# Gated mix of sliding attention and a SwiGLU layer: the tail's queues, its late rows and output, and the place of the gates

## The chip, the core and the metric

The kernel runs on one core of one Trainium2 chip. A core has TensorE (PE, matmuls), VectorE (DVE), ScalarE (ACT), GpSimd (POOL) and SyncE (SP), each with an instruction stream of its own that it executes in order. A transfer (DMA) is issued by an engine's queue, here SyncE's or GpSimd's, and carried by 16 DMA engines. An instruction that waits for a semaphore holds up everything behind it on its engine. The metric is device time in microseconds (us). Three runs gave 838.3, 838.88 and 845.08; the median is 838.88.

## The reference

Inputs in float32: x is 2048 by 512, there are 32 heads of width 16, the attention window is 256 back, the hidden width of the second layer is 1792.

```
q, k, v = split(x @ wqkv)                        # 32 heads of 16
p = softmax(mask(q k^T / 4))                     # 0 <= i - j < 256
a = (p v) @ wo
b = (silu(x @ w_gate) * (x @ w_up)) @ w_down
g = sigmoid(sum(x * gate_w, -1))                 # one number for each row
out = g * a + (1 - g) * b
```

## The kernel before

Products in full precision are made of three matmuls: each operand is split into a high half of reduced float32 and a low half (`split`, L66: a copy on one engine, a subtraction on another), and high by high, high by low and low by high are added in PSUM (`mm3`, L76). The rows are cut into four chunks of 512 (`c`), the hidden width into 14 tiles of 128 (`n` or `f`), the heads into eight groups of four (`g`).

**Opening (to about 105 us) and attention (to 616).** After the projections the kernel goes through 128 ticks (L728), 16 for each head group, each in four slots (`hd`). A slot issues a score product of the next group (`stage1`, L533, whose row maximum VectorE takes at L547 from one of two ps1 banks), a score product of this group (`stage2`, L573, exponential on ScalarE, L586, and two masks on GpSimd, L588 and L591, into `pt`), and steps of the gate and up products (`stream`, L526), which need no attention data and fill TensorE. Every fourth tick has the values' product (`av`, L596) and its evacuation (`evacuate`, L613: ScalarE copies one half to `ob`, VectorE the other to `oe`, GpSimd adds them and sends the sum to DRAM as `od`). Gate and up results are copied by ScalarE from PSUM into `ev` buffers (`kept`, L454; EV = 7 of them, taken in turn) and sent by SyncE to DRAM as `raws`. The list `AT` holds work by slot number 4 * tick + hd; `at` puts work at a slot, `later(n)` puts it n slots on, and `tick_end` runs it at the end of the slot.

In group 7 (from tick g7 = 112, about 559 us) there is no next group and `stage1` is out. There the kernel before does the gates: `gate_place` (L655) makes room in a slot of the dead query and key tiles, `gate_block` (L659) fetches 128 rows of x by SyncE and six slots later lets VectorE multiply by `gw` and sum over the row (L662), one block every three slots; `gate_end` (L665) makes the sigmoid. It fetches the down rows 0 to 7 (`wd_early`, L671, through `ev` buffers, split wholly on VectorE), loads tiles 0 to 2 of chunk 0 back from `raws` (`tile_load`, L680) and makes tile 0 ready (`tile_early`, L685); tiles 1 and 2 follow at its end (`tile_silu`, L697).

**Tail (from 616).** For each of 56 pairs (chunk, tile) the loop at L892 emits: the load of a later tile into one of four `got` buffers (`load_kept`, L831, SyncE), SiLU and product (`hidden`, L837: ScalarE L840, VectorE L841), the split of the tile before (`halved`, L844), and a down step (`step`, L853: four row blocks of three matmuls, 12 in all). In chunk 0 it also fetches and splits the down rows 8 to 13 (`load_wd`, L443, VectorE; the fetch is L277) and the four blocks of `wo` (`load_wo`, L773), and loads the softmax denominators, inverts them and stores and reloads the reciprocals, spread over rows (`load_den`, `put_den`, `load_rd`). Heads and reciprocals of a chunk (`load_oc`, L780; `load_rd`, L797) are eight transfers. `attn_step` (L824) takes two stages for each of four row blocks: `attn_split` (VectorE's product of heads and reciprocals, high half on ScalarE, low half on GpSimd), and two iterations later `attn_out` (L807: twelve matmuls with `wo` into `pb`, and the gated sum into the output buffer). When a chunk's 14 steps are done, VectorE adds its part into the output buffer and the rows are stored (`put`, L817). In the tail every transfer is in SyncE's queue, in the order in which the loop emits it; GpSimd has only the low halves of `wo` and of the attention output. The accumulators of a chunk's four blocks are the two ps1 banks, then the two ps2 banks (L856).

## Time and profile before

| what | us |
|---|---|
| median of three runs | 838.88 |
| profiled execution, its own time | 841.71 |
| its span, first to last instruction | 840.0 |
| opening, to 105 | 105 |
| opening's end and attention, 105 to 616 | 511 |
| a head group in attention's steady part | 54.7 |
| group 7, from 558.8 to the tail | 57.2 |
| tail, 616 to the span's end | 224 |

In the lines that follow, a timeline row is: start and duration in us, engine, line, operation, out<-in, sizes, count, and in brackets the engine's idle time before it with what ended that. A row with an engine's name and a q (SPq) is one of its queue. A row of windows is: the stretch and its length, then for each engine its busy time and, in parentheses, its instructions, and at the end the granted TensorE clock as a share, the DMA engines' busy share and what they moved in GB/s; the engines are PE, PEld (weight loads), DVE, ACT and POOL. Where a window is taken for one line of the kernel, only that line's engines stand in it. Matmul durations overlap, so the distance of two starts is what one takes.

### The profile page before, as it was taken

The numbers are of one execution on the slowest core, as the hardware profiler recorded it, in microseconds if no ns is written. First come the engines' busy times: TensorE is split into PE (matmuls) and PEld (weight loads), VectorE is DVE, ScalarE is ACT, GpSimd is POOL, SyncE is SP. The second block draws the span as 40 slices with busy tenths as digits, with TensorE's granted clock in tenths as the row PEclk, the third lists the DMA queues.
The fourth block names the chain that finished last, engine by engine and source line by source line (L and its number), as shares of the span: only waits on it lengthen the run. The fifth ranks groups of instructions, "written<-read, shape, count | busy, mean of one in ns | idle before, by whom it ended". The sixth has DMA issues, their size and how long they took to land. (4 is left out here: it accounts for less than half of the span.)

```text
span 840.0 us, 20730 instructions
## 1 busy us (share of the span) xinstructions
PE 816.7 (97%) x7897; PEld 687.6 (82%) x7897; DVE 542.8 (65%) x1396; ACT 468.3 (56%) x947; POOL 370.9 (44%) x659
## 2 busy tenths in 40 slices
PE   9999999999999999999999999999979799999988
PEld 7888887998888888888988888887767588878866
DVE  5675534887867677687777786757748365545453
ACT  7455452246777676676767676766653343434341
POOL 5124467136566566565756666657721121001010
PEclk9999999999999999999999999999999899999999
DMA  8446679662544365444553564339667776484751
GB/s 297 142 174 226 225 256 307 210 205 91 191 165 162 131 194 182 142 159 156 173 187 132 165 198 151 130 114 301 240 244 225 238 238 211 153 276 126 230 169 50
DMA packets 82147, 158.91 MB, mean 189 GB/s; under 512 B 12608, under 2 KB 18112, under 8 KB 82048
## 3 DMA queue, kind: packets, MB, share of 16 engines
q1 hardware_dynamic: 78080, 143.69, 52.1%
q0 software_dynamic: 3968, 13.90, 4.5%
q8 instruction: 62, 1.02, 0.5%
q14 instruction: 37, 0.30, 0.1%
HBM read 92.80 MB, written 64.75 MB: 188 GB/s over the span
## 5 line engine op out<-in xcount | busy, mean ns | idle before, releaser
L547 DVE CUSTOM_DVE_ANT_0 ps<-ps,mask 128x384 f32<-128x384 f32 (+2 forms) x512 | 273.6, 544 | 52.8 <-PE ps L545 23.6
L586 ACT ACTIVATE pt<-ps 128x384 f32<-128x384 f32 (+2 forms) x512 | 237.4, 478 | 77.2 <-PE ps L545 29.9
L584 PE MATMUL ps<-q,k 64*128 64x384 f32 (+2 forms) x512 | 164.2, 331 | 0.1
L545 PE MATMUL ps<-k,q 63*128 63x384 f32 (+2 forms) x512 | 157.4, 327 | 0.0
L588 POOL TENSOR_SCALAR_AFFINE_SELECT pt<-pt 128x256 f32<-128x256 f32 x256 | 107.3, 419 | 96.9 <-ACT pt L586 87.5
L841 DVE TENSOR_TENSOR sg<-got,sg 128x512 f32<-128x512 f32 x53 | 48.9, 922 | 82.0 <-ACT sg L840 62.8
L584 PEld LDWEIGHTS ps<-q,k 64*128 64x128 f32 x512 | 93.3, 184 | 8.7 <-ACT pt L586 4.6
L489 PE MATMUL pb<-xhi,wh 64*128 64x512 f32 x432 | 99.3, 402 | 0.0
L545 PEld LDWEIGHTS ps<-k,q 63*128 63x128 f32 x512 | 89.0, 184 | 11.7 <-DVE mx L547 0.9
L489 PE MATMUL pb<-xlo,wh 64*128 64x512 f32 x432 | 98.1, 394 | 0.0
L489 PE MATMUL pa<-xhi,wh 64*128 64x512 f32 x432 | 98.0, 400 | 0.0
L489 PE MATMUL pb<-xhi,wl 64*128 64x512 f32 x432 | 97.4, 392 | 0.0
L489 PE MATMUL pa<-xlo,wh 64*128 64x512 f32 x432 | 96.3, 394 | 0.0
L489 PE MATMUL pa<-xhi,wl 64*128 64x512 f32 x432 | 95.6, 392 | 0.0
L591 POOL TENSOR_SCALAR_AFFINE_SELECT pt<-pt 128x256 f32<-128x256 f32 x224 | 94.4, 421 | 0.0
L71 POOL TENSOR_TENSOR ol<-raw,oh 128x512 fp32r<-128x512 f32 x16 | 20.7, 1295 | 132.5 <-ACT oh L68 132.5
L608 PE MATMUL ps<-pt,vg 64*32 64x320 f32 (+4 forms) x2816 | 77.8, 348 | 1.3 <-POOL pt L588 1.2
L608 PEld LDWEIGHTS ps<-pt,vg 64*32 64x32 f32 x2816 | 50.8, 106 | 29.5 <-issue 9.4
L547 DVE DVE_READ_ACCUMULATOR2_ANT mx<- 128x1 f32 x512 | 72.3, 141 | 0.0
L621 POOL TENSOR_TENSOR oe<-oe,ob 128x512 f32<-128x512 f32 (+1 forms) x32 | 41.0, 1281 | 65.3 <-ACT ob L619 57.6
L620 DVE COPY oe<-ps 128x512 f32<-128x512 f32 x32 | 22.1, 691 | 61.7 <-issue 44.1
L489 PEld LDWEIGHTS pb<-xhi,wh 64*128 64x128 f32 x432 | 51.6, 186 | 4.9 <-issue 3.2
(226 smaller groups left out, 1677.9 us busy)
## 6 DMA issues: line engine op xcount, KB each, us to landing
raws<-ev SPq DMA_DIRECT2D x112, 256.0 KB
got<-raws SPq DMA_DIRECT2D x106, 256.0 KB
q<-xd SPq DMA_DIRECT2D x96, 128.0 KB
k<-xd SPq DMA_DIRECT2D x96, 128.0 KB
xd<-cx SPq DMA_DIRECT2D x16, 512.0 KB
xd<-cy SPq DMA_DIRECT2D x16, 512.0 KB
od<-oe POOLq DMA_DIRECT2D x32, 256.0 KB, 3.2
raw<-wgu SPq DMA_DIRECT2D x28, 256.0 KB
```

The lines of the kernel that those rows point to most:

```text
L71: lo_eng.tensor_tensor(out=lo, in0=src, in1=hi.bitcast(F32), op=ALU.subtract)
L489: mm = nc.tensor.matmul(ps[me], w[r], x[r], start=not second and i == 0, stop=bool(second) and i == n - 1)
L545: nc.tensor.matmul(ps[:, :n], QT[g % 2][pr][r, q0:q0 + P], KT[g % 2][pr][r, k0:k0 + n], start=True, stop=True)
L547: mx = nc.vector.tensor_tensor_reduce(out=ps[:, :n], in0=ps[:, :n], in1=mask[:, 3 * P - n:], scale=1.0, scalar=NEG, op0=ALU.add, op1=ALU.m ...
L584: nc.tensor.matmul(ps[:, :n], KT[g % 2][pr][r, k0:k0 + P], QT[g % 2][pr][r, k0:k0 + n], start=True, stop=True)
L586: BEHIND.append(nc.scalar.activation(pt[:, j, :n], ps[:, :n], AF.Exp, scale=SCALE))
L588: nc.gpsimd.affine_select(out=pt[:, :, :P], in_=pt[:, :, :P], pattern=[[0, 2], [1, P]], compare_op=ALU.is_ge, fill=0.0, base=0, channel_mu ...
L591: nc.gpsimd.affine_select(out=pt[:, :, 2 * P:], in_=pt[:, :, 2 * P:], pattern=[[0, 2], [-1, P]], compare_op=ALU.is_ge, fill=0.0, base=-1, ...
L608: nc.tensor.matmul(AV[g, c][h][32 * j:32 * j + 32, q0 - c * CH:q1 - c * CH], VG[4 * g + kb // 4][o, kb % 4, 17 * j:17 * j + 32], PT[g, kb, ...
L620: nc.vector.tensor_copy(e, first)
L621: nc.gpsimd.tensor_tensor(out=e[:, lo:], in0=e[:, lo:], in1=o[:, lo:], op=ALU.add)
L841: nc.vector.tensor_tensor(out=sg, in0=gu[1], in1=sg, op=ALU.mult)
```

## The change

- Gates: their blocks leave group 7. They get buffers of their own, and block b is fetched by SyncE at tick 18 + 4b and multiplied nine slots later, in groups 1 to 4 and the first tick of group 5; the sigmoid is made at tick 110.
- `ev` buffers: five for seven.
- Down rows: rows 0 to 7 are fetched at ticks 113 to 120. Rows 8 to 12 are fetched by SyncE from tick 125 on and, for two of them, right behind attention, into the buffers of the gate and up weights; row 13 by GpSimd in the tail. They are split in the tail by ScalarE and VectorE, one in each of iterations 3 to 8.
- Tiles: 0 and 1 are made ready early, the SiLU of 2 is made at the last tick and its split after it, and tile 3 is loaded at tick 127.
- Evacuation in group 7: VectorE adds ScalarE's copy to the other half from PSUM; GpSimd only sends.
- Tail, queues: SyncE's queue keeps the tiles (and the last chunk's stores); `wo`, denominators, reciprocals, heads and the other chunks' stores go into GpSimd's.
- Tail, order: tile loads come first and run four tiles ahead; denominators are asked for at its start and inverted in iterations 9 to 12; heads and reciprocals of chunks 1 to 3 come one iteration sooner.
- Attention output in four steps, each one or two iterations after the one before: divide, split, matmuls, gated sum.
- A chunk's accumulators start with the ps2 banks.

The diff, its core:

```
-EV = 7
+EV = 5
...
             nc.scalar.copy(o[:, lo:], second[:, lo:])
-            nc.vector.tensor_copy(e, first)
-            nc.gpsimd.tensor_tensor(out=e[:, lo:], in0=e[:, lo:], in1=o[:, lo:], op=ALU.add)
+            if g == G - 1:
+                nc.vector.tensor_tensor(out=e[:, lo:], in0=first[:, lo:], in1=o[:, lo:], op=ALU.add)
+                if lo:
+                    nc.vector.tensor_copy(e[:, :lo], first[:, :lo])
+            else:
+                nc.vector.tensor_copy(e, first)
+                nc.gpsimd.tensor_tensor(out=e[:, lo:], in0=e[:, lo:], in1=o[:, lo:], op=ALU.add)
...
+        gwb = osb.tile([P, D], F32, name="gwb")
+        nc.sync.dma_start(gwb, gw[None, :].to_broadcast([P, D]))
         def gate_block(b):
-            gwb, t = GT[0], GT[1 + b % 3]
+            t = osb.tile([P, D], F32, name="xn", bufs=2)
             nc.sync.dma_start(t, xn[b * P:(b + 1) * P])
-            later(6, lambda: nc.vector.scalar_tensor_tensor(t, t, 1.0, gwb, op0=ALU.mult, op1=ALU.mult,
+            later(9, lambda: nc.vector.scalar_tensor_tensor(t, t, 1.0, gwb, op0=ALU.mult, op1=ALU.mult,
...
-        RAW_AT, TILE_AT = (14, 8, 14), (12, 10, 13)
+        RAW_AT, TILE_AT = (14, 8, 14, 8), (12, 10, 13)
...
+        for b in range(NB):
+            at(4 * (18 + 4 * b) + 2, lambda b=b: gate_block(b))
+        at(4 * (g7 - 2), gate_end)
         at(4 * g7, put_pieces)
         for m in range(8):
-            wd_early(4 * (g7 + 1 + m + m // 6 * 6) + 2, m, m)
+            wd_early(4 * (g7 + 1 + m) + 2, m, m)
...
-        early = tile_early(0)
-        for n in range(6):
-            at(4 * (g7 + 10) + 3 + 3 * n, lambda: run(early, 1))
-        at(4 * (g7 + NB - 2) + 3, lambda: tile_load(2, RAW_AT[0]))
-        at(4 * g7, gate_place)
-        for b in range(NB):
-            at(4 * g7 + 1 + 3 * b, lambda b=b: gate_block(b))
-        at(4 * (g7 + NB - 1), gate_end)
+        early = chain(tile_early(0), tile_early(1))
+        for n in range(12):
+            at(4 * (g7 + 10) + 3 + 2 * n, lambda: run(early, 1))
+        at(4 * (g7 + 13), lambda: tile_load(2, RAW_AT[2]))
+        at(4 * (g7 + 15) + 3, lambda: tile_load(3, RAW_AT[3]))
+        def wd_raw(f, name):
+            WDRAW[f] = ring.tile([P, D], F32, name=name, bufs=1 if name == "raw" else 2)
+            nc.sync.dma_start(WDRAW[f], wd[f])
+        for f, (i, name) in enumerate(((13, "raw"), (13, "wh"), (13, "wl"), (17, "wh"), (17, "wl")), 8):
+            at(4 * (g7 + i) + 2, lambda f=f, name=name: wd_raw(f, name))
...
+        def split_wd(f):
+            WD[f] = halves_of(pieces[f])
+            split(*WD[f], WDRAW.pop(f), nc.scalar, nc.vector)
...
+        def attn_divide(c, b):
+            HOLD[c, b] = o = by_k(raw2())
+            cols = slice(b * P, (b + 1) * P)
+            nc.vector.tensor_tensor(out=o, in0=OC[c][:, :, cols], in1=RD[c][:, :, cols], op=ALU.mult)
         def attn_split(c, b):
             oh, ol = (by_k(bp.tile([P, D], F32R, name=w)) for w in ("oh", "ol"))
+            split(oh, ol, HOLD[c, b], *act)
+            HOLD[c, b] = oh, ol
...
-            nc.sync.dma_start(out[0, t * P:(t + 1) * P], ga)
+            nc.gpsimd.dma_start(out[0, t * P:(t + 1) * P], ga)
+        def attn_step(c, n):
+            for b, f in ((n - 3, attn_out), (n - 4, attn_put), (n - 1, attn_split), (n, attn_divide)):
+                if 0 <= b < 4:
+                    f(c, b)
...
-                ACC[c] = [pool.tile([P, D], F32, name=name) for pool, name in ((ps1, "ps1"), (ps2, "ps2")) for _ in range(2)]
+                ACC[c] = [pool.tile([P, D], F32, name=name) for pool, name in ((ps2, "ps2"), (ps1, "ps1")) for _ in range(2)]
...
+        ready = [load_wo(k) for k in range(3)]
+        for c in range(NCH):
+            load_den(c)
+        GOT[0, 3] = GOT[3]
+        loads = seq[4:]
...
+            if c == 0:
+                if n == 4:
+                    WDRAW[13] = ring.tile([P, D], F32, name="raw", bufs=1)
+                    nc.gpsimd.dma_start(WDRAW[13], wd[13])
+                if n < 9:
+                    split_wd(n + 5)
+                else:
+                    if n < 13:
+                        ready.pop(0)()
+                        put_den(n - 9)
+                    if n == 9:
+                        ready.append(load_wo(3))
+                    if n >= 10:
+                        load_oc(0, n - 10)
+            elif n < 4:
+                load_oc(c, n)
+            if c == 0 and n >= 10:
+                load_rd(0, n - 10)
+            elif c and n < 4:
+                load_rd(c, n)
+            if c == 1:
+                attn_step(0, n - 1)
+            if c > 1 and n == 0:
+                attn_step(c - 1, 7)
+            if c:
+                attn_step(c, n - 7)
```

In `load_wo`, `load_oc`, `load_den`, `put_den` and `load_rd`, too, `nc.sync.dma_start` becomes `nc.gpsimd.dma_start`.

## What was predicted before the run

> **What bounds the kernel now.** I read the page first (busy shares, slices), then TensorE's timeline in the tail, then the queues behind its gaps, then the attention stage.
>
> ```profile
> PE 816.7 (97%) x7897; PEld 687.6 (82%) x7897; DVE 542.8 (65%) x1396; ACT 468.3 (56%) x947; POOL 370.9 (44%) x659
> ...
> PE   9999999999999999999999999999979799999988
> ```
>
> TensorE (PE) is the bound; only slices in the tail (from 616) show it short of work. Its timeline there, every idle time of note:
>
> ```profile
> 618.03 0.50 PE L80 MATMUL ps<-q,k 128*128 128x512 f32 x1 [1.68 <-ACT ob L619]
> ...
> 630.07 0.60 PE L82 MATMUL ps<-q,hl 128*128 128x512 f32 x1 [3.14 <-DVE hl L71]
> 630.47 0.63 PE L80 MATMUL ps<-q,hh 128*128 128x512 f32 x1
> 630.90 0.63 PE L81 MATMUL ps<-q,hh 128*128 128x512 f32 x1
> ...
> 643.56 0.50 PE L82 MATMUL ps<-k,hl 128*128 128x512 f32 x1 [0.71 <-DVE hl L71]
> ...
> 666.91 0.80 PE L80 MATMUL ps<-k,hh 128*128 128x512 f32 x1 [5.62 <-ACT hh L68]
> ...
> 751.99 0.50 PE L80 MATMUL ps<-k,hh 128*128 128x512 f32 x1 [0.81 <-ACT hh L68]
> ...
> 800.56 0.50 PE L80 MATMUL ps<-k,hh 128*128 128x512 f32 x1 [1.53 <-ACT hh L68]
> 802.01 0.50 PE L82 MATMUL ps<-k,hl 128*128 128x512 f32 x1 [0.72 <-DVE hl L71]
> 805.43 0.51 PE L80 MATMUL ps<-k,hh 128*128 128x512 f32 x1 [0.86 <-ACT hh L68]
> ```
>
> After a long gap the next starts are 0.43 apart (630.47 to 630.90), so a gap costs more than its length. What the tail could save at most:
>
> ```profile
> 616.08:836.20 220.12, 203.90 (x882) 163.68 (x868) 113.05 (x158) 84.46 (x148) 27.71 (x22) 0.98 0.63 200
> 616.40:630.00 13.60, 8.91 (x38) 7.06 (x38) 6.33 (x10) 5.68 (x11) 1.85 (x2) 1.00 0.89 314
> 710.00:730.00 20.00, 20.00 (x90) 16.58 (x89) 7.86 (x11) 8.12 (x15) 1.56 (x2) 1.00 0.39 118
> 800.00:806.00 6.00, 3.86 (x14) 2.40 (x14) 2.39 (x4) 1.65 (x3) 0.00 (x0) 1.00 0.91 286
> ```
>
> The undisturbed stretch 710 to 730 has 89 weight loads in 20.0 us, 0.225 each; the tail's 868 would take about 195 of its 220 us. Some 22 to 24 us are idle or slow. By place, each with its slow restarts: handover from attention 1.7; steps 3 to 11 of chunk 0, 7.3 (3.14, 0.71 and smaller gaps, 4.5 in all, and 2.8 of slow starts); boundary of chunks 0 and 1, 8.2 (5.62 and 2.6 slow); boundaries 1/2 and 2/3, 5.5 (0.81, 1.53, 0.72, 0.86 and 1.6 slow). The last column but one is the DMA share: 0.89 and 0.91 where TensorE starves, 0.39 where it does not.
>
> **Tail, opening (7.3).** The longest early gap comes through VectorE, which sits behind a late down row:
>
> ```profile
> 627.66 0.43 DVE L70 CAST q<-raw 128x512 fp32r<-128x512 f32 x1 [4.55 <-DMA raw<-wd]
> ```
>
> This cast is in VectorE's order ahead of the product and split that the next down step needs. Now rows 8 to 12 are asked for in attention, row 13 four steps ahead, and tile 3 comes before the tail too; the split uses ScalarE for its first half. What is late next: tiles 4 to 6 on SyncE, which share the DMA engines with rows 11 and 12, three `wo` rows and the denominators. A tile is two transfers:
>
> ```profile
> got<-raws SPq DMA_DIRECT2D x106, 256.0 KB
> ```
>
> With tile 3, two last stores of attention and rows of the same size that is sixteen transfers and the denominators, 4.4 MB from about 613; at the 314 GB/s shown, 14 us, so until 627, and tile 6 is needed for step 5 near 628. It is close: I keep 1.3 as a remaining stall, -6.0, between 0 and -7.3.
>
> **Handover (1.7).** The first step waited for the last evacuation's ScalarE copy in a ps1 bank. It now opens in ps2, free since the last exponential. -1.7, between 0 and -1.7. VectorE now adds straight from PSUM in group 7, after the ScalarE copy; the next user of ps1 is half a step away (six matmuls by 0.225, 1.35 us), about what copy and add need, so I cost it at nothing.
>
> **Boundaries (8.2 and 5.5).** SyncE's queue around the third one, and VectorE beside it:
>
> ```profile
> 766.40 10.39 SPq L835 DMA_DIRECT2D got<-raws  x6
> ...
> 781.41 2.37 SPq L822 DMA_DIRECT2D out<-k  x4
> 783.88 2.24 SPq L835 DMA_DIRECT2D got<-raws  x2
> ```
>
> ```profile
> 795.10 0.69 DVE L841 TENSOR_TENSOR sg<-got,sg 128x512 f32<-128x512 f32 x1 [4.18 <-DMA got<-raws]
> ...
> 800.66 0.69 DVE L841 TENSOR_TENSOR sg<-got,sg 128x512 f32<-128x512 f32 x1 [4.27 <-DMA got<-raws]
> ```
>
> The four stores wait for the chunk's end on TensorE; behind them no tile is asked for from 776.8 to 783.9. That is 7 us of lead lost while heads and reciprocals (1 MB per two steps) crowd in, and VectorE then waits 4.18 and 4.27 for tiles. With stores, heads and reciprocals in GpSimd's queue, SyncE waits only for a tile buffer. So 5.5 goes entirely. At boundary 0/1 there is no store in the way: chunk 0's and chunk 1's heads and reciprocals, 16 transfers of 256 KB, fall into some eight steps with tiles of 512 KB each. 8.4 MB at the 286 GB/s shown is 29 us against 8 steps of 12 matmuls, 22 us; a lead of about four tiles (11 us) covers most of it. -5.5 of 8.2, between +8 and -8.2. The price in GpSimd's queue:
>
> ```profile
> L622 POOL DMA_DIRECT2D od<-oe x32: 557/557/582, 194.8 to 619.6; - x32
> ...
> DMA to landing us min/median/max: 2.3/3.2/6.1
> ```
>
> A chunk has 12 such issues, 6.7 us, and GpSimd was busy 27.7 in the tail's 220: there is room. Queued behind its waits are the lower halves of the attention output; with output in four steps each stands two steps (5.4 us) ahead of its matmuls, so cover for a wait of that length and no more. The added lag also lets ScalarE and VectorE read a finished product instead of waiting for the one just issued.
>
> **Group 7 (gain).** Windows counted by the score matmuls of attention's second stage (64 are a head group, 16 or so four ticks):
>
> ```profile
> 504.02:558.79 54.77, 21.00 (x64) 11.79 (x65) 1.00 0.41 135
> ...
> 572.00:584.94 12.94, 4.57 (x17) 2.76 (x17) 1.00 0.93 308
> 584.94:600.92 15.98, 4.63 (x17) 2.67 (x17) 1.00 0.75 259
> ```
>
> ```profile
> 588.27 0.85 POOL L588 TENSOR_SCALAR_AFFINE_SELECT pt<-pt 128x256 f32<-128x256 f32 x1
> ...
> 589.89 0.40 POOL L588 TENSOR_SCALAR_AFFINE_SELECT pt<-pt 128x256 f32<-128x256 f32 x1
> ```
>
> ```profile
> 590.34 0.53 PE L608 MATMUL ps<-pt,vg 64*32 64x64 f32 x22 [0.85 <-POOL pt L588]
> ```
>
> Four ticks of group 7 took 15.98 where the four before took 12.94: the values waited for GpSimd's masks, which take 0.85 instead of 0.40 while VectorE runs gate products and row splits. The gates leave, and GpSimd's evacuation adds too. -2.9, between 0 and -4. What comes in (a second early tile with its long reciprocal; five `ev` buffers for seven) meets no queue that TensorE waits for: a buffer is asked for again five uses later, and SyncE may wait a few us with a value load that is six ticks early.
>
> **Gates in groups 1 to 4 (cost).** The 16 products land behind the last score of a tick that has the values, hence in front of the next scores' maxima:
>
> ```profile
> 262.72 0.57 DVE L547 CUSTOM_DVE_ANT_0 ps<-ps,mask 128x384 f32<-128x384 f32 x1
> ...
> 263.37 0.57 DVE L547 CUSTOM_DVE_ANT_0 ps<-ps,mask 128x384 f32<-128x384 f32 x1
> ```
>
> ```profile
> 263.64 0.34 PE L545 MATMUL ps<-k,q 63*128 63x384 f32 x1
> 264.28 0.34 PE L545 MATMUL ps<-k,q 63*128 63x384 f32 x1
> ```
>
> ```profile
> 262.10 1.30 POOL L621 TENSOR_TENSOR oe<-oe,ob 128x512 f32<-128x512 f32 x1 [2.26 <-ACT ob L619]
> ```
>
> ```profile
> 599.49 0.69 DVE L662 SCALAR_TENSOR_TENSOR k<-k 128x512 f32<-128x512 f32 x1 [0.46 <-DMA k<-xn]
> 600.11 0.08 DVE L662 DVE_READ_ACCUMULATOR k<-k 128x1 f32 x1
> ...
> 605.86 1.79 DVE L662 SCALAR_TENSOR_TENSOR k<-k 128x512 f32<-128x512 f32 x1
> ```
>
> ```profile
> 605.48 1.62 POOL L621 TENSOR_TENSOR oe<-oe,ob 128x512 f32<-128x512 f32 x1 [2.47 <-ACT ob L619]
> ```
>
> Both engines are full there: a maximum every 0.65, a score every 0.64, and scores have two banks. The score at 264.28 needs the bank of the maximum begun at 263.37, done at 263.94: 0.34 ahead, part of it signalling. I take half, 0.17, as slack. A free gate product holds VectorE 0.62 (599.49 to 600.11), so TensorE loses 0.45, which nothing gives back, since it is the bound. Sixteen of them and the gate's end (three short instructions at tick 110, priced as one more): 17 by 0.45 is +7.6. Bounds: 0.28 each if all 0.34 is slack, +4.8; 1.62 each if the product has to sit out GpSimd's add (1.79, less 0.17), +27.5. I take the near one: the product would start at 263.37 and the add ends at 263.40. Their transfers, 256 KB each four ticks, are asked for nine slots ahead.
>
> One rule speaks against this placement: by the Trainium skill, SBUF — State Buffer, section "Who interferes with whom", a VectorE instruction with two SBUF inputs and a GpSimd instruction that reads SBUF exclude each other, and whichever began first keeps the port. The trace agrees: the product at 605.86 ended 0.55 after the add at 605.48 did. By the rule a product that starts after the add waits for its end, at worst all 1.3 us and rival (c)'s 844.8; by the rows at 262 to 264 it waits 0.03, and the sum is the 824.9 below.
>
> **The sum.** -1.7 - 6.0 - 5.5 - 5.5 = -18.7 in the tail, -2.9 in group 7, +7.6 for gates: -14.0. Against the profiled execution (span 840.0, time 841.71) that is 826.0 and 827.7; the median of the runs shown is 838.88, 2.83 below it, so 824.9.
>
> **Rivals.** (a) Two queues starve the tiles: GpSimd's queue is not held back by tile buffers, so its bursts take half of the DMA engines just where the share is 0.91. If that doubles the boundaries' 13.7, the tail gives -7.7 + 13.7 = +6.0, and the whole +10.7: 849.6, slower. It decides once the boundaries lose more than 16.7. For it: 0.91; against it: 0.39 in mid chunk, where lead is built again. The Trainium skill, DMA: Bandwidth & Descriptors, section "Queues, rings and completion order", says that a DMA engine goes round its queues packet by packet, which is this mechanism; no run yet shows two busy queues. (b) The boundaries are short of DMA, not of issues, and stay at 13.7: -7.7 - 2.9 + 7.6 = -3.0, 835.9. (c) Each gate sits out the add: -18.7 - 2.9 + 27.5 = +5.9, 844.8. (d) Scores absorb the gates and nothing is left of the tail's loss: -22.7 - 2.9 = -25.6, 813.3.
>
> **Chances.** Forecast 0.50, (a) 0.12, (b) 0.20, (c) 0.08, (d) 0.10. A measurement tells about 1% (8.4 us) from no change. The forecast's own range is 817 to 833; a fifth of it lies within 1%. Faster: 0.40 of the forecast, 0.10 of (d) and 0.03 of (b), should it come out better than priced: 0.53. Slower: (a) and 0.01 of (c), 0.13. Same: what is left, 0.34. The range leaves out (a) and the outer half of (d): 814 to 844.
>
> **What would show it.** Right: TensorE idle under 5 us after 616; no gap at 626 or 660; tile loads without a pause at chunk ends; group 7 near 54; groups 1 to 4 longer by 1.8 each than the 54.77 of group 6. Wrong: VectorE waiting for `got` or heads at chunk boundaries (a, b); gate products of 1.8 us beside GpSimd's add (c); groups 1 to 4 unchanged (d).

## The result and the profile after

The changed kernel takes 835.26 us (median of 15 executions, 833.36 to 837.79), the kernel before 839.86 (median of 15). The ratio is 0.9943, with a 95% interval of 0.9929 to 0.9956: 4.8 us off by this ratio, where 14 were forecast. Every median here leaves out one execution, of run 16 below, that took 886.68 us at a granted clock of 0.851. The profiled execution has a span of 833.8 against 840.0, so 6.2 less, and the account below is made against these spans.

The page of the changed kernel, busy shares and TensorE's slices:

```profile
PE 816.1 (98%) x7897; PEld 684.0 (82%) x7897; DVE 541.6 (65%) x1394; ACT 471.0 (56%) x953; POOL 398.7 (48%) x712
...
PE   8999999999999999999999999999999979999997
```

One slice of the tail is still short of work, the 33rd (667 to 688); the second trough of before, around 800, is gone. Windows cut at the same places of both programs: start of group 7, first down step, down step 12 of chunk 0, first down step after chunk 0's first output block, end. Before:

```profile
558.79:618.03 59.24, 56.25 (x802) 44.72 (x799) 37.47 (x67) 40.13 (x92) 39.58 (x71) 1.00 0.65 222
618.03:658.41 40.38, 35.87 (x145) 27.91 (x145) 25.84 (x39) 15.04 (x26) 5.72 (x5) 0.96 0.84 265
658.41:680.30 21.89, 16.04 (x62) 12.28 (x60) 7.69 (x10) 8.95 (x16) 2.56 (x2) 0.84 0.73 231
680.30:840.00 159.70, 151.72 (x664) 123.49 (x662) 79.06 (x108) 58.53 (x103) 19.42 (x15) 1.00 0.56 179
```

After:

```profile
565.90:621.20 55.30, 55.29 (x803) 44.63 (x801) 25.79 (x36) 39.87 (x90) 32.73 (x68) 1.00 0.51 170
621.20:656.25 35.05, 33.34 (x150) 26.98 (x145) 26.51 (x37) 20.08 (x38) 17.86 (x26) 1.00 0.99 329
656.25:679.62 23.37, 16.53 (x61) 13.10 (x60) 8.97 (x11) 7.67 (x13) 7.94 (x11) 0.78 1.06 241
679.62:833.80 154.18, 149.79 (x664) 123.97 (x662) 78.72 (x104) 57.61 (x101) 35.57 (x42) 1.00 0.57 172
```

Row by row, against before: group 7 with the handover takes 3.9 less, the opening of the tail 5.3 less, and the last row ("from chunk 1 on" below; it begins with step 16, the third of chunk 1) 5.5 less. The third row, boundary 0/1, grew by 1.5 in these two executions. Five of the runs below (1, 2, 6, 13 and 14) do the same work as the changed kernel in the tail until this stretch ends, and it takes 20.9 to 24.6 in them. So the 1.5 is within the spread, and what is sure is that the stretch did not shrink by 5.5. The last row is steadier, 153.8 to 154.2 in the four of them whose tail is wholly unchanged (1, 2, 13 and 14). Group 7 begins 7.1 later than before (565.90 against 558.79): those are the gates, plus 0.2 from ahead of group 1. The sum is +7.1 - 3.9 - 5.3 + 1.5 - 5.5 = -6.1 (-6.2 before rounding).

Where the third row loses it, TensorE's timeline of the changed kernel:

```profile
664.63 0.39 PE L81 MATMUL ps<-q,hh 128*128 128x512 f32 x1
671.86 0.80 PE L82 MATMUL ps<-q,hl 128*128 128x512 f32 x1 [6.84 <-DVE hl L71]
672.45 0.63 PE L80 MATMUL ps<-q,hh 128*128 128x512 f32 x1
672.88 0.63 PE L81 MATMUL ps<-q,hh 128*128 128x512 f32 x1
```

It waits for `hl`, a split by VectorE. VectorE's timeline there:

```profile
656.88 0.69 DVE L71 TENSOR_TENSOR hl<-sg,hh 128x512 fp32r<-128x512 f32 x1 [1.42 <-ACT hh L68]
669.91 0.69 DVE L820 TENSOR_TENSOR raw<-xhi,xhi 128x512 f32<-128x512 f32 x1 [12.34 <-DMA xlo<-rd]
670.52 0.68 DVE L862 TENSOR_TENSOR sg<-got,sg 128x512 f32<-128x512 f32 x1
671.12 0.69 DVE L71 TENSOR_TENSOR hl<-sg,hh 128x512 fp32r<-128x512 f32 x1
```

The reader should see the order. VectorE did nothing for 12.34 us because the next instruction of its stream was L820, the first division of chunk 0's attention output, which waited for reciprocals (the profile names the one that landed last before it; the division needs all of chunk 0's, the last of which was issued at 655.73 and landed 13.9 us later). The product (L862) behind it waited for nothing of its own, and neither did the split: each ran as soon as the division was done. The division feeds matmuls two steps later; the split behind it feeds the next step. A transfer that nobody needed yet held up work that was due.

Why the reciprocals were late: GpSimd's timeline, where they are issued, and the landing of all L813 issues (minimum, median, maximum):

```profile
646.94 0.64 POOL L813 DMA_DIRECT2D xhi<-rd  x1
...
655.73 0.59 POOL L813 DMA_DIRECT2D xhi<-rd  x1 [0.72 <-DMA xhi<-rd]
...
659.09 0.59 POOL L813 DMA_DIRECT2D xlo<-rd  x1 [2.19 <-DMA xhi<-od]
```

```profile
DMA to landing us min/median/max: 6.9/10.0/16.1
```

And the queues between 648 and 680, packets, MB, share of 16 engines, with the median landing in the last column:

```profile
q0 software_dynamic: 2380, 4.35, 58.1%
q1 hardware_dynamic: 1924, 3.50, 45.4%
...
xlo<-od POOLq DMA_DIRECT2D x4, 256.0 KB, 14.2
xlo<-rd POOLq DMA_DIRECT2D x4, 256.0 KB, 14.6
```

The DMA engines are hardly ever without a packet (58.1% and 45.4%, 104% together, since packets of the two queues overlap) and the two queues move about as much each. A transfer of 256 KB that landed after 3.2 us in attention takes 7 to 16 here. GpSimd itself is held up as well: from 654 on it waits before most issues until an earlier transfer has landed.

### The profile page after: what moved, and what is told of

The parts are those of the page before. It is cut to its first block, busy times and chain, and to the rows that moved or that the text cites. A ratio compares the mean times of both kernels' runs of the same rounds, so it can differ in the third digit from the quotient of the medians.

```text
span 833.8 us, 20786 instructions
## 1 busy us (share of the span) xinstructions
PE 816.1 (98%) x7897; PEld 684.0 (82%) x7897; DVE 541.6 (65%) x1394; ACT 471.0 (56%) x953; POOL 398.7 (48%) x712
## 4 chain that ended last, share of the span: by engine, by line
PE 88%; DMA 5%; DVE 4%; POOL 1%; ACT 1%; issue 1%; SPq 0%; DVEq 0%; ACTq 0%; POOLq 0%
PE pa L489 17%; PE pb L489 17%; PE ps L608 9%; PE ps L545 6%; PE ps L584 5%; PE ps L82 5%; PE ps L81 5%; PE ps L80 4%; PE ps L371 4%; PE pa L371 3%; PE ps L209 3%; PE pb L371 3%; DVE ps L547 2%; PE pb L81 2%; PE pb L80 2%; DMA got<-raws 2%
## 5 line engine op out<-in xcount | busy, mean ns | idle before, releaser
L545 PE MATMUL ps<-k,q 63*128 63x384 f32 (+2 forms) x512 | 159.2, 331 | 1.9 <-DVE mx L547 0.4
L862 DVE TENSOR_TENSOR sg<-got,sg 128x512 f32<-128x512 f32 x52 | 45.1, 866 | 47.3 <-ACT sg L861 35.6
L626 POOL TENSOR_TENSOR oe<-oe,ob 128x512 f32<-128x512 f32 (+1 forms) x28 | 35.3, 1262 | 54.1 <-ACT ob L619 50.4
L625 DVE COPY oe<-ps 128x512 f32<-128x512 f32 x28 | 19.4, 692 | 60.0 <-issue 43.5
L71 POOL TENSOR_TENSOR ol<-raw,oh 128x512 fp32r<-128x512 f32 x16 | 22.5, 1409 | 67.0 <-ACT oh L68 66.8
```

What stands on the lines that cost most here:

```text
L545: nc.tensor.matmul(ps[:, :n], QT[g % 2][pr][r, q0:q0 + P], KT[g % 2][pr][r, k0:k0 + n], start=True, stop=True)
L862: nc.vector.tensor_tensor(out=sg, in0=gu[1], in1=sg, op=ALU.mult)
```

## The experiments

Runs 1, 3, 15 and 16 were executed four or five times, the others once. Single times say little, since 15 executions of the changed kernel lie between 833.36 and 837.79; the readings go by windows and waits of the profiled execution.

### Gates: is the loss VectorE's lateness behind the values' product?

**1, `e1_gates_before_values`:** the product moves from the last slot of its tick to the second, ahead of the values.

```
-            later(9, lambda: nc.vector.scalar_tensor_tensor(t, t, 1.0, gwb, ...
+            later(7, lambda: nc.vector.scalar_tensor_tensor(t, t, 1.0, gwb, ...
```

> The changed kernel with one number altered: the gate product is put seven slots after its fetch instead of nine, so in VectorE's order it stands just ahead of a values product, where VectorE was idle for over 2 us, and no longer behind the last score of that tick. Theory A (the gates cost time because VectorE is full right after the values): the ticks of 3.12 to 3.18 us go back to 2.80, groups 1 to 5 from 55.3 to 56.4 back to 54.7 to 54.8, and the whole is 5 to 6 us shorter than the changed kernel, span near 828. Theory B (it is the product itself, its transfer or its use of the port beside GpSimd's masks, wherever it stands): groups 1 to 4 stay near 56.2 and the span near 834.

Measured 829.58, ratio 0.9864 (0.9849 to 0.9878), 5.7 below the changed kernel's median. Its first down step begins at 616.1 instead of 621.2. Group 1 of this kernel, then of the changed one:

```profile
230.97:285.77 54.80, 54.80 (x772) 47.20 (x770) 43.14 (x143) 38.01 (x84) 34.31 (x71) 1.00 0.56 181
```

```profile
230.59:286.57 55.98, 55.69 (x772) 47.03 (x770) 42.31 (x144) 38.04 (x83) 33.83 (x72) 1.00 0.56 176
```

The gates cost next to nothing two slots earlier, with the same products, buffers and transfers. What they cost was their place: VectorE comes out of the values' tick with maxima due, and TensorE has two score banks.

**2, `e2_gates_in_group7`:** the gates go back into group 7, with five `ev` buffers as changed.

```
-            at(4 * (18 + 4 * b) + 2, lambda b=b: gate_block(b))
-        at(4 * (g7 - 2), gate_end)
+            at(4 * g7 + 1 + 3 * b, lambda b=b: gate_block(b))
+        at(4 * (g7 + NB - 1), gate_end)
...
-            later(9, lambda: nc.vector.scalar_tensor_tensor(t, t, 1.0, gwb, ...
+            later(6, lambda: nc.vector.scalar_tensor_tensor(t, t, 1.0, gwb, ...
```

> The changed kernel with the gates put back into group 7, one block every three slots and multiplied six slots later, the sigmoid at its end, but in the new buffers (two in turn, where the kernel before had three). Theory A (the gates in group 7 caused the stall of GpSimd's masks there): groups 1 to 6 go back to 54.7, 7.4 us less in all, and the third four ticks of group 7 go from 13.8 to about 16, group 7 3 us longer; span near 829.5. Theory B (GpSimd's evacuation add caused that stall, and it is gone either way): group 7 stays near 55 to the first down step, span near 826.5.

Measured 837.37. Groups 1 to 6 are back at 54.7 to 55.1, but group 7 with the handover takes 62.3, 7 more than as changed. ScalarE's timeline and TensorE's in this kernel:

```profile
585.35 0.59 ACT L516 COPY ev<-pb 128x512 f32<-128x512 f32 x1 [2.38 <-DVE q L71]
585.83 0.88 ACT L586 ACTIVATE pt<-ps 128x384 f32<-128x384 f32 x2
```

```profile
586.38 0.82 PE L584 MATMUL ps<-q,k 64*128 64x384 f32 x2 [3.94 <-ACT pt L586]
```

With five buffers ScalarE's copies wait for VectorE to split the down rows that sit in them, VectorE now has the gates too, and the exponentials stand behind the copies. So fewer buffers are affordable only because the gates left. The third four ticks take 15.24, neither theory's 13.8 nor the old stall: the loss is another wait, of 1.20 at their last tick, to which run 14 comes back.

### Boundary 0/1: VectorE's order, the queue, or the amount of data?

**3, `e3_late_divide`:** chunk 0's four output steps come two iterations later.

```
-                attn_step(0, n - 1)
+                attn_step(0, n - 3)
```

> The changed kernel with the attention output of chunk 0 two iterations later (its first division at the fourth step of chunk 1 instead of the second). Theory A (the stall at 664 is VectorE's order: the division waits for the reciprocals of chunk 0, and the next step's split stands behind it; the tiles are there): the 6.8 us gap shrinks to under 2, and the span is 7 to 9 us shorter, 825 to 827. Theory B (the DMA engines are short there and TensorE would starve for tiles two steps later): the gap moves by two steps and keeps 5 us or more, span 832 to 834.

Measured 830.59, ratio 0.9884 (0.9866 to 0.9902); four executions took 827.75 to 832.43, and the profile is of the fastest. VectorE's and TensorE's timelines of this kernel:

```profile
670.15 0.69 DVE L820 TENSOR_TENSOR raw<-xhi,xhi 128x512 f32<-128x512 f32 x1 [3.12 <-DMA xlo<-rd]
```

```profile
672.10 0.50 PE L82 MATMUL ps<-q,hl 128*128 128x512 f32 x1 [0.23 <-DVE hl L71]
```

The reciprocals land when they did (the division starts at 670.15, as changed at 669.91), and yet the gap is 0.23 for 6.84. The transfers are as late as before; only what stands behind the wait has changed. From the first down step to the end it takes 203.9 for the changed kernel's 212.6. By the medians the gain is 4.7, so the other executions seem to have got less of it; why is not known.

**4, `e5_heads_sync`:** heads and reciprocals return to SyncE's queue, all else as changed.

```
-            nc.gpsimd.dma_start(OC[c][:, k], heads[:, :DH, c * CH:(c + 1) * CH])
+            nc.sync.dma_start(OC[c][:, k], heads[:, :DH, c * CH:(c + 1) * CH])
...
-            nc.gpsimd.dma_start(RD[c][:, k], rd[c, 8 * k:8 * k + 8][:, None].to_broadcast([8, DH, CH]))
+            nc.sync.dma_start(RD[c][:, k], rd[c, 8 * k:8 * k + 8][:, None].to_broadcast([8, DH, CH]))
```

> The changed kernel with heads and reciprocals of all chunks back in SyncE's queue, each behind the tile asked for in the same iteration; stores, wo and denominators stay in GpSimd's. Theory A (chunk 0's reciprocals are late because GpSimd's queue gets only half of the DMA engines, the other half going to tiles that run four ahead): in one queue they stand behind fewer tiles, the wait of the first division falls from 12.3 us to under 7, the gap at the boundary 0/1 from 6.8 to 2 to 4, span 828 to 831. Theory B (the volume alone decides): gap and span as in the changed kernel, 6 to 8 us and 833 to 835. Beside it: if the boundaries 1/2 and 2/3 get their gaps back (over 2 us in all), it was heads leaving SyncE's queue that saved them, else the earlier tile loads.

Measured 829.07. The division's wait shrinks from 12.34 to 8.25 and it starts 5 us sooner; the gap is 2.75:

```profile
664.76 0.69 DVE L820 TENSOR_TENSOR raw<-xhi,xhi 128x512 f32<-128x512 f32 x1 [8.25 <-DMA xlo<-od]
```

Between 648 and 680 as much passes as in the changed kernel (7.99 MB in all, 7.87 there), now nearly all in one queue:

```profile
q1 hardware_dynamic: 4175, 7.82, 78.4%
q0 software_dynamic: 70, 0.16, 1.4%
```

The same data at the same rate; what differs is whose turn comes when. In the loop's own order the eight transfers of chunk 0 land sooner, beside half of the engines they land later. So the new queue made the loss larger, and the order on VectorE made it a loss. That this is more than the spread shows in the other runs: runs 7 and 8, with the heads in SyncE's queue too, have gaps of 2.25 and 1.93, while the six kernels that leave this stretch as changed have 4.77 to 8.36.

**5, `e6_half_tiles`:** tiles 16 to 23 load only their gate part, which stands in for the up part too, so eight tiles carry half of their data and those products are not the reference's.

```
+            if 16 <= NF * c + f < 24:
+                t = got.tile([P, CH], F32, name="got0")
+                GOT[c, f] = [t, t]
+                nc.sync.dma_start(t, raws[f, 0, c])
+                return
```

> The changed kernel with half the tile traffic where chunk 0's heads are loaded: of eight tiles (16 to 23) only the gate part is loaded and used as the up part too, so the output is not the reference's. Theory A (tiles and heads share saturated DMA engines): some 1 MB less goes in front of the last reciprocals, at 240 GB/s 4 us, the gap of 6.8 us falls to 2 to 4. Theory B (the heads' transfers themselves are slow, by their pattern or by GpSimd's issue): they land as late as before and the gap stays at 6 to 8.

Measured 833.74, gap 4.54, the division's wait 10.05. Between the two expectations, and hardly outside the spread given under run 4 (the wait there is 10.28 at the least). So whether 2 MB less of tiles helps at all, one execution cannot show; it is in any case far less than the order on VectorE did.

### The later boundaries: the predicted reason tried

**6, `e4_stores_sync`:** the output stores return to SyncE's queue.

```
-            nc.gpsimd.dma_start(out[0, t * P:(t + 1) * P], ga)
+            nc.sync.dma_start(out[0, t * P:(t + 1) * P], ga)
```

> The changed kernel with the output rows' stores back in SyncE's queue; all else stays in GpSimd's. Theory A (stores in SyncE's queue stop the tile loads at the chunk ends, and moving them saved the 5.5 us at the boundaries 1/2 and 2/3): those gaps come back, 3 to 5.5 us in all, span 837 to 839. Theory B (the longer lead, tile loads emitted first, is what saved them): no gap comes back, span near 834.

Measured 837.7. No gap at 1/2 or 2/3, though the four stores are again among the tiles. (Boundary 0/1 has 8.36; up to there this kernel asks for the same transfers as the changed one, so that is spread.)

**7, `e9_all_sync`:** runs 4 and 6 together.

> Heads, reciprocals and output stores all go back to SyncE's queue; the tiles keep the changed kernel's order, one tile further ahead. Theory A (queue): mixing them with the tiles in one queue in order is what cost the old kernel its gaps at 1/2 and 2/3: gaps of 0.8 to 1.5 us come back there, 4 to 6 us in all. Theory B (order of issue): the tile asked for one step earlier and the output in four steps are what saved those boundaries, so still no gap after 690. At 0/1 both expect a short gap of 2 to 5 us, as with the heads alone in SyncE's queue (2.75). Time 829 to 832 under B, 833 to 837 under A.

Measured 831.99. From chunk 1 on:

```profile
676.74:830.30 153.56, 149.79 (x664) 123.97 (x662) 77.45 (x104) 57.69 (x101) 18.86 (x14) 1.00 0.58 179
```

153.6 against 154.2 as changed and 159.7 before: moving heads, reciprocals and stores to GpSimd's queue is not needed to save the later boundaries.

**8, `e12_all_sync_lead3`:** run 7, with one tile of lead less.

```
-        for _ in range(3):
+        for _ in range(2):
             load_kept(*loads.pop(0))
```

> As the run with all three kinds in SyncE's queue, and the tiles asked for one step later, as in the kernel before (one initial load fewer). Theory B1 (the extra tile of lead saved the later boundaries): gaps of 0.8 to 1.5 us at 1/2 and 2/3 come back. Theory B2 (the output's four spaced steps and the lag did it, VectorE no longer waiting on its own fresh input): no gap there. At 0/1 and at steps 3 to 6 a longer loss than with the extra tile is possible under both.

Measured 832.07; 155.6 from chunk 1 on, with one gap of 1.04 at boundary 2/3. The tile of lead is worth 2.1 of the 5.5.

**9, `e13_output_two_steps`:** run 8, with the attention output in two steps as before.

```
-            for b, f in ((n - 3, attn_out), (n - 4, attn_put), (n - 1, attn_split), (n, attn_divide)):
-                if 0 <= b < 4:
-                    f(c, b)
+            if 0 <= n - 2 < 4:
+                attn_out(c, n - 2)
+                attn_put(c, n - 2)
+            if 0 <= n < 4:
+                attn_divide(c, n)
+                attn_split(c, n)
...
-            if c == 1:
-                attn_step(0, n - 1)
-            if c > 1 and n == 0:
-                attn_step(c - 1, 7)
-            if c:
-                attn_step(c, n - 7)
+            if c == 1 and 2 <= n < 8:
+                attn_step(0, n - 2)
+            if c and n >= 8:
+                attn_step(c, n - 8)
```

> The run with all three kinds in SyncE's queue and the tiles one step later, with the attention output also in two steps as in the kernel before (division and split in one step, product and its use two steps on). From the start of step 16 to the end that run took 155.6 us, the changed kernel 154.2, the kernel before 159.7. Theory A (the spaced steps removed what the earlier tile did not): 159 to 160 here, with gaps of 0.8 to 1.5 us at 1/2 and 2/3. Theory B (something else in the tail did): stays at 155 to 156.

Measured 829.43, 155.3 from chunk 1 on. Theory A fell: the spaced steps had not saved these boundaries either. This run has neither the new queue for heads and stores nor the new steps, and took less time than the changed kernel in the one run made of it. SyncE's queue at boundary 2/3 in it shows what is left of the change there:

```profile
762.65 0.60 SPq L798 DMA_DIRECT2D xlo<-od  x1
...
768.11 0.61 SPq L798 DMA_DIRECT2D xlo<-od  x1
...
772.62 2.37 SPq L844 DMA_DIRECT2D out<-k  x4
...
776.09 0.61 SPq L798 DMA_DIRECT2D xlo<-od  x1
```

Two of the chunk's four heads go ahead of the stores. In the kernel before it was one:

```profile
776.85 0.60 SPq L783 DMA_DIRECT2D xlo<-od  x1
...
786.16 0.60 SPq L783 DMA_DIRECT2D xlo<-od  x1
```

Between these two rows stand its four stores, at 781.41.

**10, `e14_two_steps_alone`:** run 9's edit on the changed kernel itself.

> The changed kernel with the attention output in two steps as before, and nothing else undone; chunk 0's first division comes one step (2.7 us) later than in the changed kernel. Theory A (spaced steps are needed): gaps at 1/2 and 2/3 of 3 us or more in all, from step 16 to the end 157 or more. Theory B (any one of lead, queue and steps is enough): 154 to 155. The gap at 0/1 shrinks by about 2.7 of its 6.84 under both, since the division waits less.

Measured 832.1, 154.2 from chunk 1 on, and a gap of 3.38 at 0/1 in place of 6.84, since the division comes a step later.

**11, `e15_heads_step_later`:** run 9, with heads and reciprocals of chunks 1 to 3 one iteration later, as before.

```
-            elif n < 4:
-                load_oc(c, n)
+            elif 1 <= n < 5:
+                load_oc(c, n - 1)
...
-            elif c and n < 4:
-                load_rd(c, n)
+            elif c and 1 <= n < 5:
+                load_rd(c, n - 1)
```

> The run with one queue, tiles one step later and the output in two steps (155.3 us from step 16 to the end), with the heads and reciprocals of chunks 1 to 3 asked for one down step later as well, as in the kernel before. In the kernel before one pair of the four stands ahead of a chunk's four stores in SyncE's queue and three behind them with the tiles; in the run so far two and two. Theory A (the place of the heads against the stores is the rest): gaps of 0.8 to 1.5 us at 1/2 and 2/3 again, 158.5 to 160 us from step 16 to the end. Theory B (it is not): 155 to 156.

Measured 832.6. The old gaps are back, TensorE's timeline:

```profile
744.11 0.50 PE L80 MATMUL ps<-k,hh 128*128 128x512 f32 x1 [1.22 <-ACT hh L68]
...
796.50 0.50 PE L80 MATMUL ps<-k,hh 128*128 128x512 f32 x1 [1.42 <-ACT hh L68]
```

```profile
671.45:830.90 159.45, 152.03 (x664) 123.36 (x662) 78.94 (x108) 58.59 (x103) 19.40 (x15) 1.00 0.58 181
```

159.5 is the old 159.7. So one iteration's earlier issue of eight transfers for each chunk saves 4.2 of the 5.5 here, with the stores in SyncE's queue.

**12, `e16_heads_later_lead4`:** run 11 with the tile of lead again (`range(3)`).

> The same with the tile asked for one step earlier, as in the changed kernel. Theory A1 (either the tile of lead or the earlier heads is enough): 154 to 156 us from step 16 to the end, no gap over 0.5. Theory A2 (both are needed): 157 or more, gaps again at 2/3.

Measured 833.57, 157.6 from chunk 1 on, with gaps of 0.40 to 0.62 at both boundaries. The tile of lead alone takes 1.8 off; it does not replace the earlier heads.

### Group 7's old stall

**13, `e7_evac_gpsimd`:** GpSimd adds in group 7's evacuation again (`if g == G:` for `if g == G - 1:`).

> The changed kernel with group 7's evacuation as in the other groups: VectorE copies, GpSimd adds. Theory A (the stall of 2.9 us in group 7 came from VectorE's gate products slowing GpSimd's masks): group 7 stays as in the changed kernel, its third four ticks at 13.7 to 13.9, span within 1 us of it but for up to 1 us more at the handover. Theory B (GpSimd's add kept the masks late): the third four ticks go back to 15 to 16.

Measured 836.89; the third four ticks take 13.7, as in the changed kernel.

**14, `e11_gates_and_evac`:** runs 2 and 13 together.

> Gates in group 7 again and GpSimd adding the evacuation's halves there again, with five buffers as changed. Neither alone brought back the old stall in the third four ticks (15.98 in the old kernel, 13.7 to 13.8 with either one). Theory A (they caused it together, through GpSimd's masks slowed beside VectorE's products): the third four ticks take 15 to 16. Theory B (something else that moved, the early down rows, caused it): 13.5 to 14. Both expect the stall on the five buffers at the sixth tick (about 7 us) to stay, and 837 to 841 in all.

Measured 834.95. The third four ticks take 15.15, but not in the old place: no tick waits for the masks, and the loss is a wait at tick 11 that run 2 has as well, beside the one for buffers at tick 6. The expectation put run 2's third four ticks at 13.7 to 13.8; they take 15.24, so GpSimd's add on top of the gates makes them no longer. ScalarE's timeline of this run:

```profile
604.36 0.63 ACT L691 ACTIVATE ev<-k 128x512 f32<-128x512 f32 x1 [1.32 <-DMA k<-raws]
```

The sigmoid of the second early tile waits for its load, which SyncE issued behind rows of x for the gates, and the exponentials stand behind the sigmoid. The old stall did not return; two others took its place.

### The version that follows

**15, `e8_both`:** runs 1 and 3 together.

> The changed kernel with both one-number edits: the gate products just ahead of a values product, and chunk 0's attention output two iterations later. If the two losses are independent they add: 6.6 and 7.8 us off the span, near 820, and a time near 821.5, ratio to the kernel before 0.976 to 0.981. If an earlier start of the tail meets later data and a gap opens somewhere else, 823 to 828.

Measured 821.69 (five executions), ratio 0.976 (0.9732 to 0.9787): the two losses at least add up, 13.6 off the changed kernel's median against 5.7 and 4.7. The first down step begins at 616.4 and the rest takes 203.4. TensorE's slices have no trough in the tail, only 1.14 and 0.74 at step 3:

```profile
PE   9999999999999999999999999999999999999997
```

**16, `e10_both_heads_sync`:** run 15 with run 4's edit.

> The version with earlier gates and later division, with heads and reciprocals in SyncE's queue in addition. If the late landing in GpSimd's queue still costs anything there, it gets 0.5 to 2 us faster than that version's 821.7; if the later division already covers it, the same within 1 us; if the tiles lose their lead to 16 more transfers in their queue, slower by 2 or more with gaps at a chunk boundary.

Measured 822.44 (three executions), ratio 0.9777 (0.9734 to 0.982): no difference from run 15 that is clear of the spread. A gap of 2.16 opens at 681.22 where run 15 has none. Once the division is late enough, the queue of the heads makes no difference to the time that these runs can show.

## Why the prediction was wrong, point by point

The forecast was -14.0 against the span, -6.2 came. Of the 7.8 between, 7.0 are one term.

| term | predicted | measured |
|---|---|---|
| handover and group 7 | -1.7 and -2.9 | -3.9 together |
| gates | +7.6 | +6.9 |
| opening of the tail | -6.0 | -5.3 |
| boundary 0/1 | -5.5 | +1.5 (-1.0 to +2.7 in the runs with the same tail up to there) |
| boundaries 1/2 and 2/3 | -5.5 | -5.5 |

**Boundary 0/1 is the step that failed**, in "-5.5 of 8.2, between +8 and -8.2". The working priced the boundary by volume: 8.4 MB in 22 us, and a lead of four tiles that covers most of it. In neither kernel does the profile show a wait for a tile behind this gap. In the kernel before, the 5.62 came through ScalarE's timeline:

```profile
665.20 0.62 ACT L68 CAST woh<-raw 128x512 fp32r<-128x512 f32 x1 [8.86 <-DMA raw<-wo]
665.73 0.62 ACT L840 ACTIVATE sg<-got 128x512 f32<-128x512 f32 x1
```

The cast of the last row of `wo`, which no step needed yet, waited for its transfer, and the SiLU (L840) and the cast of `hh` that the next step needed stood behind it. The change asks for three rows of `wo` at the start of the tail, and on ScalarE at most 1.06 of this kind of wait is left there. Whether tiles would have been late next in the kernel before, these rows do not say. VectorE's wait for chunk 0's reciprocals took its place, and the working had no term for it. It counted what cover GpSimd's low halves have, "each stands two steps (5.4 us) ahead of its matmuls, so cover for a wait of that length and no more", and not what stands behind the division on VectorE. The landing that it showed, 2.3/3.2/6.1, is that of stores in attention. It never asked what heads and reciprocals would read beside a saturated tile queue: L813 reads 6.9/10.0/16.1 in the tail. The prediction's own sign of being wrong, VectorE waiting for heads at a chunk boundary, is what the trace shows. VectorE's wait began at 657.57 (656.88 + 0.69); TensorE had work until 664.86, 7.3 us later, and could go on at 671.86, when division, product and split were through. Run 3 took the wait out of VectorE's way and the gap went, with the transfers as late as ever; its steps 12 to 15, 48 matmuls, take 10.88, 0.227 each, so nothing is lost there. Run 4 took the new queue away and the gap fell to 2.75. The measured value lies inside the bounds that the text gave the term; the choice between them was wrong.

Rival (a) described part of it, at one boundary of three. Its mechanism is seen: 4.35 MB in one queue and 3.50 in the other in the same 32 us. The Trainium skill, DMA: Bandwidth & Descriptors, section "Queues, rings and completion order", has a DMA engine go round its queues packet by packet; the trace is in line with it, with 55% and 45% of the bytes. But what it starved were the heads, not the tiles, and it did not reach the 16.7 from which it would have decided. Rival (b) gave 835.9, nearly what was measured, by another sum: it kept all 13.7 of the boundaries, of which 5.5 went and 8.2 became 9.7. That it came so near is luck.

**Boundaries 1/2 and 2/3: the number was right, the reason was not borne out.** The text put the loss on the stores in SyncE's queue. With them there again (runs 6 and 7) no gap returned. What saved these boundaries is when things are asked for: run 11 undid the earlier heads and lost 4.2, run 8 undid the tile of lead and lost 2.1. The prediction listed neither as a gain of its own there, and its third piece, that the added lag helps, is worth nothing here: run 9 against run 8 is 155.3 against 155.6. The stores can still matter beside late heads, since there three of the four heads stand behind them; late heads with the stores in GpSimd's queue were not run, so that share stays open.

**Gates: right, mechanism and size.** In the changed kernel VectorE, TensorE and GpSimd around one gate product:

```profile
263.90 0.75 DVE L664 SCALAR_TENSOR_TENSOR xn<-xn,gwb 128x512 f32<-128x512 f32 x1
...
264.59 0.55 DVE L547 CUSTOM_DVE_ANT_0 ps<-ps,mask 128x384 f32<-128x384 f32 x1
```

```profile
264.33 0.34 PE L545 MATMUL ps<-k,q 63*128 63x384 f32 x1
265.26 0.44 PE L545 MATMUL ps<-k,q 63*128 63x384 f32 x1
```

```profile
262.81 1.30 POOL L626 TENSOR_TENSOR oe<-oe,ob 128x512 f32<-128x512 f32 x1 [2.26 <-ACT ob L619]
```

The score starts 0.93 after the one ahead of it instead of 0.64, and from group 1 to the start of group 7 6.9 us are lost, 0.40 for each of the 17 places, against 0.45 priced. Rival (c) is out: the product starts 0.21 before the add ends and takes 0.75. All sixteen (minimum, median, maximum in ns):

```profile
L664 DVE SCALAR_TENSOR_TENSOR xn<-xn,gwb x16: 689/748/1173, 249.5 to 460.7; 128x512 f32<-128x512 f32 x16
```

The Trainium skill, SBUF — State Buffer, section "Who interferes with whom", would have the product wait for the add's end. These 0.21 are all that the rule can ask for at this place, and the 0.75 is only 0.06 over the shortest. So this row does not show the rule at work; whether it speaks against it hangs on when the add had read its last input, which the row does not tell. Rival (d), that scores absorb it, is out for this placement and true for run 1's.

**Opening: right in size, at another place.** What would be left was priced at 1.3, for tile 6 and step 5. About 2 were left, and the gaps, 1.14 and 0.57, are at step 3. ScalarE's timeline there:

```profile
629.60 0.63 ACT L861 ACTIVATE sg<-got 128x512 f32<-128x512 f32 x1 [5.95 <-DMA got<-raws]
```

SyncE asks for tile 4, the first of the tail, only at 623.03, and the cast of `hh` for step 3 stands behind this SiLU of tile 4: once more an order loss. No run took the early down rows or the early tile back, so which of them brought the gain was not tested.

**Group 7 and handover: right in sum, cause open.** The third four ticks take 13.76 for 15.98, TensorE busy throughout:

```profile
592.03:605.79 13.76, 13.75 (x187) 10.90 (x184) 5.52 (x7) 9.73 (x22) 7.46 (x18) 1.00 0.48 180
```

The text put this on the gates leaving, with the evacuation beside it. Run 2 brought the gates back, run 13 the evacuation, run 14 both, and in none did the values wait for masks. The wait may hang on how gates, down rows 6 and 7 and the buffers fell together in the kernel before; that was not settled. What the runs do show is that gates in group 7 with five buffers and a second early tile cost 7 us there, so moving them was needed for a reason that the prediction had not named ("meets no queue that TensorE waits for").

## What to carry to other kernels

Price a transfer that moves to another queue at its landing beside the traffic of the place it moves to, and compare that with the distance from the first instruction that waits for it, not from the one that needs its result. In an engine's stream a wait for something that is due late belongs behind the work that is due first: two iterations of delay for the division and two slots less for the gates took 4.7 and 5.7 us off the median here, each about as much as the whole change had (4.6), and both together 13.6. When a gain has come out as forecast, undo its supposed cause all the same; here it was another line of the same diff.

## What the runs showed of the hardware that was not expected

- Two busy queues took more of the DMA engines' time for the same bytes, and moved no more of them. Between 648 and 680 GpSimd's queue took 58.1% for 4.35 MB and SyncE's 45.4% for 3.50 MB, 13.4 and 13.0% per MB; in run 4 SyncE's alone took 78.4% for 7.82 MB, 10.0% per MB. In all it was 7.87 and 7.99 MB. A DMA share near 1 is thus no measure of what the engines could move: 0.99 went with 329 GB/s in the opening of the tail and 1.06 with 241 at boundary 0/1. That packets of the two queues wait for one another would explain it; no run shows that directly.
- From 654 to 665 GpSimd waits 0.33 to 2.50 us before six of its issues until an earlier transfer has landed, as the profile's releasers have it. An engine that issues transfers can be held up by the transfers themselves; why these issues wait is not shown.
- After the gap of 6.84 the next matmuls start 0.43 apart for more than 5 us, until 677.57, and then 0.23 again. The third row (656.25 to 679.62) has a granted clock of 0.78. At 0.225 each its 60 weight loads would take 13.5 of its 23.37, and the gap takes 6.84: the other 3.0 is what the gap cost beyond its own length.
